# Turning four columns of final sums on VectorE in blocks of 32, with a store of sixteen short runs

## The chip, the cores and the metric

The kernel runs on one core of a Trainium2 chip. The metric is the device time of one execution in microseconds. A core has five engines that run their own programs and wait for one another through semaphores: PE (TensorE, matrix products and transposes), DVE (VectorE), ACT (ScalarE), POOL (GpSimd) and SP (SyncE, which here issues most of the transfers). Sixteen DMA engines move data between the memory (HBM) and the on-chip memory SBUF; PE writes its results to a second on-chip memory, PSUM.

## The reference

One decoding step of a layer with two branches, mixed by a gate g. Branch a is attention of one new position over a cache of 4096 positions with 32 heads of 128; branch b is a small network with a squared ReLU. Everything is bfloat16.

```python
def _A_ref(x, k_cache, v_cache, wq, wo):      # x: 1 x 1 x 512, caches: 1 x 32 x 4096 x 128
    q = (x @ wq).reshape(B, Sq, Hq, Dh) ...
    scores = jnp.einsum("bhqd,bhkd->bhqk", q, k) * (Dh ** -0.5)
    p = _softmax(scores, axis=-1)
    o = jnp.einsum("bhqk,bhkd->bhqd", p, v)
    return ... @ wo                            # 4096 -> 512
def _B_ref(x, w1, b1, w2, b2):
    h = x @ w1 + b1                            # 512 -> 1376
    r = jnp.where(h > 0, h, 0)
    return (r * r) @ w2 + b2                   # 1376 -> 512
g = _sigmoid((x * gate_w).sum(-1, keepdims=True))
return g * a + (1 - g) * b                     # 1 x 1 x 512
```

## The kernel before

The heads are handled in eight groups of four (q = 0 to 7). For each group SP loads 4 MB of keys and 4 MB of values into two slots each, in an order that is written out by hand (ORDER); the weights wq, w1, wo and w2 are put between them. Twelve of every 32 key blocks are multiplied and summed on DVE (L685, L689); the others are transposed on PE (L460), copied out by ACT (L355) and multiplied on PE (L467). ACT computes the exponentials (L372), PE the products with the values (L501). PE's program is a loop of named pieces with branches.

The 512 outputs are summed in `acc`, four columns of 128 partitions in PSUM: output number 128 j + p stands in column j of partition p. The output projection (`out_rows`, L534) and the second layer of the network (`mlp_out`, L545) add to these columns with one matmul for each column and each block of weights. The last piece of w2 to be needed is the last load that SP issues, and the store waits behind it on SP.

The end of the kernel, which the change touches, is one line of steps. DVE adds the bias columns b2g to acc and writes `accs`, 128 x 4 in bfloat16 (L756). PE transposes accs into four rows of 128 in PSUM, `acc4` (L646). DVE copies these to SBUF, `fin4` (L758). SP, which waits for that at L281, stores fin4 as four rows of 256 B from partitions 0 to 3 (L282). After the block of the engines' programs has ended (L760), SP waits for the store to land (L761), and the program is over. The semaphores on the way are s_acc (last matmul done), s_as (accs written), s_fin (transposed), s_f4 (fin4 written) and s_out (stored).

Of the kernel before, what the change touches and what calls it, by code (L numbers as in the profile page):

```python
# [5 lines left out]
def bass_gated_mix__gqa_block_cached__dense_activation_squared_relu__decode_kernel(  # L6
# [16 lines left out]
    bf16 = mybir.dt.bfloat16  # L23
# [56 lines left out]
    with ctx:  # L80
        def sb(name, shape, dt):
            return ctx.enter_context(nc.sbuf_tensor(name, shape, dt))

        def pb(name, shape, dt):
            return ctx.enter_context(nc.psum_tensor(name, shape, dt))

        def sem(name):
            return ctx.enter_context(nc.semaphore(name))
# [21 lines left out]
        b2r = w1_sb[0:4, 2, 0:128]  # L110
        oT = sb("oT", [GH, 128], bf16)
        o2 = sb("o2", [128, TB], bf16)
        fin4 = sb("fin4", [4, 128], bf16)
        zeros = sb("zeros", [128, 128], bf16)
        xb = sb("xb", [128, 4, 128], bf16)
        ident = sb("ident", [128, 128], bf16)
# [21 lines left out]
        accs = sb("accs", [128, 4], bf16)  # L138
# [4 lines left out]
        pO = pb("pO", [128, 512], fp32)  # L143
# [7 lines left out]
        O2 = KP[3][:, 0:2 * TB].bitcast(fp32)  # L151
        Z = pO[:, 76:77]
        B2 = pO[:, 78:80].bitcast(bf16)
        acc4 = pO[0:4, 128:192].bitcast(bf16)
        QR = [pQ[:, :]] + [p[:, :].bitcast(fp32) for p in KP[0:3]] + [pQ[:, :]] * (NQ - QF)
        H = KP[0][:, 0:2 * (FG + 1)].bitcast(fp32)
        acc = pQ[:, 256:260]
# [53 lines left out]
        s_oc = sem("s_oc")  # L211
        s_acc = sem("s_acc")
        s_as = sem("s_as")
        s_fin = sem("s_fin")
        s_f4 = sem("s_f4")
        s_out = sem("s_out")

# [11 lines left out]
        @block.sync  # L229
        def _(eng):  # L230
            def load_kv(n):
                kind, q = ORDER[n]
                if q >= 2:
                    done(kind, q - 2)
                if kind == "K":
                    eng.dma_start(KV[:, K_SLOT[q], :], k_q[q, :, :]).then_inc(s_k[q], 16)
                else:
                    at = 0
                    for m, sv in zip(V_PARTS[q], s_v[q]):
                        a, b = at * PB * 128, (at + m) * PB * 128  # L240
                        eng.dma_start(KV[:, V_SLOT[q], a:b], v_q[q, :, a:b]).then_inc(sv, 16)  # L241
                        at += m

            def done(kind, q):
                if kind == "K":
                    eng.wait_ge(s_sd, NP * (q + 1))
                    eng.wait_ge(s_t, GQ * (q + 1))
                else:
                    eng.wait_ge(s_pv, q + 1)

            def load_wo(g):
                if g == 0:
                    eng.wait_ge(s_qps, NQ)
                elif g < NG - 1:
                    eng.wait_ge(s_wd, g)
                a = 0 if g < NG - 1 else 1
                eng.dma_start(wo_sb[:, a, :, :], wo_v[g, :, :, :]).then_inc(s_wo[a], 16)  # L257

            def load_w2(n):
                a, b = W2_PARTS[n]  # L260
                if a < FG:
                    eng.dma_start(w2a[:, a:b, :], w2_v[:, a:b, :]).then_inc(s_w2[n], 16)  # L262
                else:
                    eng.dma_start(w2b[:, :], B_w2[FG * 128:F, :]).then_inc(s_w2[n], 16)  # L264

            for n in range(len(ORDER)):
                load_kv(n)
                if n == 2:
                    eng.wait_ge(s_z, 1)
                    eng.wait_ge(s_b2, 1)  # L270
                    eng.dma_start(w1_sb[:, :, :], w1_v[:, :, :]).then_inc(s_w1, 16)
                if n in WO_AT:
                    load_wo(WO_AT[n])
            load_wo(NG - 1)
            eng.wait_ge(s_sd, NP * NQ)
            load_w2(0)
            load_w2(1)
            load_w2(2)
            load_w2(3)
            load_w2(4)  # L280
            eng.wait_ge(s_f4, 1)  # L281
            eng.dma_start(out[0, 0, :].rearrange("(j p) -> j p", p=128), fin4[:, :]).then_inc(s_out, 16)  # L282


        @block.gpsimd
# [122 lines left out]
        def _(eng):  # L408
# [129 lines left out]
            def mlp_out(c, last=False):  # L538
                eng.wait_ge(s_w2[c], 16)
                a, b = W2_PARTS[c]  # L540
                for n in range(a, b):
                    M = 128 if n < FG else FR
                    w = w2a[:, n, :] if n < FG else w2b[:, :]
                    for j in range(4):
                        mm = eng.matmul(acc[:, j:j + 1], w[:, j * 128:(j + 1) * 128], hs[0:M, n:n + 1],  # L545
                                        start=False, stop=last, skip_group_check=True)
                if last:
                    mm.then_inc(s_acc, 1)
# [93 lines left out]
            mlp_out(2)  # L642
            mlp_out(3)
            mlp_out(4, last=True)
            eng.wait_ge(s_as, 1)
            eng.transpose(acc4, accs[:, :], ident[:, :]).then_inc(s_fin, 1)  # L646


        @block.vector
        def _(eng):  # L650
# [103 lines left out]
            eng.wait_ge(s_acc, 1)  # L754
            eng.wait_ge(s_bg, 1)
            eng.tensor_tensor(accs[:, :], acc[:, 0:4], b2g[:, :], ALU.add).then_inc(s_as, 1)  # L756
            eng.wait_ge(s_fin, 1)
            eng.tensor_copy(fin4[:, :], acc4).then_inc(s_f4, 1)  # L758

        body.close()  # L760
        nc.sync.wait_ge(s_out, 16)  # L761
# [28 lines left out]
```

## Time and profile before

| what | value |
|---|---|
| time, median of 3 runs | 190.87 us (190.75 to 190.93) |
| time of the profiled execution | 190.55 us |
| its span | 189.2 us |
| mean granted TensorE clock | 0.735 |
| busy: PE, DVE, ACT, POOL | 137.1, 123.0, 116.0, 6.0 us |
| DMA | 78.47 MB, mean 415 GB/s |
| packets under 512 B, of all | 483 of 4177 |

The span runs from the first to the last instruction of the profiled execution; its device time is 1.35 us longer. Busy times of engines overlap and don't add up to the span. In the profile's lines a step is named by the line of the kernel, the engine, and the tiles that it writes and reads; buffer numbers are left out, so fin4 is shown as fin.

### The profile page before, as it was taken

How to read it: one execution, taken by the hardware profiler on the slowest of the kernel's cores; microseconds unless marked ns; L12 is line 12 of the kernel's file. 1: busy time of each engine (PE TensorE's matmuls, PEld its weight loads, DVE VectorE, ACT ScalarE, POOL GpSimd, SP SyncE). 2: the span in 40 equal slices, each digit the busy share in tenths (PEclk: the TensorE clock that was granted, in tenths of full speed). 3: DMA queues.
4: the chain of work that ended last, by engine and by line, in shares of the span. 5: the costliest groups of instructions: out<-in, count | busy, mean ns of one | idle time of the engine just before them, and what ended most of it. 6: DMA issues, size and time to landing. Idle time of an engine off the chain costs nothing. (4 is left out here: it accounts for less than half of the span.)

```text
span 189.2 us, 6234 instructions
## 1 busy us (share of the span) xinstructions
PE 137.1 (72%) x2688; PEld 119.8 (63%) x2688; DVE 123.0 (65%) x123; ACT 116.0 (61%) x243; POOL 6.0 (3%) x13
## 2 busy tenths in 40 slices
PE   0009297668849979969968797829868496889865
PEld 0003165537739779758958696829767495879864
DVE  0110099979969999996998299919990499701010
ACT  3004559948989986984987099708973298560000
POOL 4000000000700000000000000000000000000000
PEclk9999969958975975995795559655985579555555
DMA  6999999989989999999999999999999999999992
GB/s 225 437 444 443 443 443 426 443 361 483 440 360 436 443 443 440 417 436 430 443 424 409 423 443 443 436 436 436 414 445 409 416 443 443 438 388 416 421 388 78
DMA packets 4177, 78.47 MB, mean 415 GB/s; under 512 B 483, under 2 KB 837, under 8 KB 1094
## 3 DMA queue, kind: packets, MB, share of 16 engines
q1 hardware_dynamic: 4152, 78.32, 97.1%
q8 instruction: 7, 0.11, 0.2%
q14 instruction: 4, 0.03, 0.0%
q10 hardware_dynamic: 14, 0.01, 0.0%
HBM read 78.32 MB, written 0.00 MB: 414 GB/s over the span
## 5 line engine op out<-in xcount | busy, mean ns | idle before, releaser
L355 ACT ACTIVATE kT<-KP 128x1024 bf16<-128x1024 bf16 x80 | 75.3, 1041 | 26.1 <-PE KP L460 25.9
L685 DVE TENSOR_TENSOR w2a<-KV,qb 128x1536 f32<-128x1536 bf16 x32 | 56.3, 1760 | 19.4 <-DMA KV<-in_A_k_cache_dram 19.0
L460 PE MATMUL KP<-ident,KV 128*128 128x128 bf16 x640 | 59.6, 256 | 10.5 <-PEq L455 10.5
L460 PEld LDWEIGHTS KP<-ident,KV 128*128 128x128 bf16 x640 | 48.4, 116 | 14.1 <-issue 13.1
L689 DVE TENSOR_REDUCE S<-w2a 128x12 f32<-128x1536 f32 x32 | 56.1, 1753 | 1.1
L467 PE MATMUL pS<-qc,kT 128*128 128x4 bf16 x640 | 28.1, 166 | 13.0 <-PEq L455 11.0
L467 PEld LDWEIGHTS pS<-qc,kT 128*128 128x128 bf16 x640 | 24.6, 99 | 18.9 <-issue 17.6
L501 PEld LDWEIGHTS pO<-E,KV 128*128 128x128 bf16 x1024 | 29.3, 105 | 0.0
L501 PE MATMUL pO<-E,KV 128*128 128x4 bf16 x1024 | 28.4, 166 | 0.0
L372 ACT ACTIVATE E<-S,nM 32x128 bf16<-32x128 f32 x32 | 18.5, 578 | 0.9
L445 PE MATMUL pQ<-W,xb 128*128 128x512 bf16 x20 | 7.8, 532 | 7.2 <-DMA W<-in_A_wq_dram 6.1
L338 ACT ACTIVATE qb<-pQ 32x128 bf16<-32x128 f32 x20 | 5.4, 268 | 9.7 <-PE pQ L445 9.3
L361 ACT ACTIVATE S<-pS 32x80 f32<-32x80 f32 x32 | 7.3, 228 | 4.8 <-PE pS L467 4.2
L445 PEld LDWEIGHTS pQ<-W,xb 128*128 128x128 bf16 x20 | 2.2, 126 | 9.6 <-DMA W<-in_A_wq_dram 6.2
L372 ACT ACTIVATION_READ_ACCUMULATOR E<-S,nM 32x1 f32 x32 | 8.1, 252 | 0.0
L664 DVE TENSOR_SCALAR e<-ez 128x1 f32<-128x1 f32 x1 | 0.2, 153 | 10.8 <-ACT ez L387 10.8
L708 DVE RECIPROCAL rden<-pO 128x4 f32<-128x4 f32 x8 | 1.4, 174 | 8.2 <-PE pO L501 8.2
L594 PE MATMUL pO<-ident,w_sb 1*128 1x1 bf16 x4 | 0.3, 165 | 7.8 <-DMA w_sb<-in_A_x_dram 7.8
L497 PE MATMUL pO<-RS,onesf 128*128 128x4 f32 x16 | 4.3, 339 | 1.8 <-PEq L455 1.8
L655 DVE TENSOR_SCALAR xb<-zeros,xcolf 128x128 bf16<-128x128 bf16 x4 | 0.7, 248 | 7.5 <-ACT xcolf L331 7.5
L488 PE MATMUL pM<-identf,mp 128*1 128x128 f32 x8 | 3.0, 372 | 3.4 <-PEq L455 3.1
L497 PEld LDWEIGHTS pO<-RS,onesf 128*128 128x128 f32 x16 | 3.8, 298 | 2.1 <-issue 2.0
(75 smaller groups left out, 72.2 us busy)
## 6 DMA issues: line engine op xcount, KB each, us to landing
KV<-in_A_k_cache_dram SPq DMA_DIRECT2D x8, 4096.0 KB, 22.0
KV<-in_A_v_cache_dram SPq DMA_DIRECT2D x7, 4096.0 KB, 29.5
W<-in_A_wq_dram SPq DMA_DIRECT2D x1, 4096.0 KB, 13.4
W<-in_A_wo_dram SPq DMA_DIRECT2D x4, 1024.0 KB, 16.5
KV<-in_A_v_cache_dram SPq DMA_DIRECT2D x1, 2048.0 KB, 11.0
KV<-in_A_v_cache_dram SPq DMA_DIRECT2D x2, 1024.0 KB, 14.1
w_sb<-in_B_w_dram SPq DMA_DIRECT2D x1, 1376.0 KB, 24.4
w2a<-in_B_w_dram SPq DMA_DIRECT2D x2, 512.0 KB, 18.5
```

Of the source, the lines that this page charges most:

```text
L338: eng.activation(qb[rows(r), c, :], QR[c][rows(r), r * 128:(r + 1) * 128], ACT.Copy)\
L355: eng.activation(kT[:, n % NT, :], KP[n % NKP][:, :], ACT.Copy).then_inc(s_ev, 1)
L361: eng.activation(S[rows(r), q % NS, 0:YQ], S2[rows(r), :, r], ACT.Copy).then_inc(s_cp, 1)
L372: eng.activation(E[rows(r), q % 2, :, r], S[rows(r), q % NS, :], ACT.Exp, bias=nM[rows(r), q:q + 1], scale=SCALE, accum_out=RS[rows(r), q ...
L445: mm = eng.matmul(QR[c], xb[:, t, :], wq_sb[:, t, c * 512:(c + 1) * 512], start=(t == 0), stop=(t == 3))
L460: mm = eng.transpose(KP[(GQ * a + g) % NKP][:, y * 128:(y + 1) * 128], key(a, b), ident[:, :])
L467: mm = eng.matmul(pS[:, R * c:R * c + R], kT[:, (GQ * a + g) % NT, y * 128:(y + 1) * 128], qc2[:, a, :], start=True, stop=True)
L488: eng.transpose(MT, mp[:, a:a + 1], identf[:, :]).then_inc(s_mt, 1)
L497: eng.matmul(DEN[a], onesf[:, :], RS[:, a, :], start=True, stop=True)
L501: mm = eng.matmul(O[a], KV[:, V_SLOT[a], b * 128:(b + 1) * 128], E[:, a, COLUMN[b], :], start=(b == 0), stop=(b == NB - 1))
L685: eng.tensor_tensor(prod, KV[:, K_SLOT[q], x:x + XB * 128].rearrange("p (b d) -> p b d", d=128), qb[:, q, :].unsqueeze(1).to_broadcast([12 ...
L689: eng.tensor_reduce(S[:, q % NS, c:c + XB], prod, AX.X, ALU.add).then_inc(s_sd, 1)
```

## The change

DVE does the turning. It has a transpose of its own that turns each square block of 32 partitions x 32 elements by itself. Its input here is accs with every column read 32 times (an access with a step of zero), which makes 128 partitions x (4 x 32) elements; its output is `fin`, 128 x 128. After it, every partition of block a (partitions 32 a to 32 a + 31) holds, for each column j, the 32 values that stood in column j of that block's partitions. Of these equal rows one for each block is stored: partitions 0, 32, 64 and 96. Each holds four pieces of 32 outputs (64 B) that belong at four places of the output, 256 B apart, so the store consists of 16 runs. The transpose on PE, its semaphore s_fin, the PSUM columns acc4 and the copy to fin4 are gone.

```diff
-        fin4 = sb("fin4", [4, 128], bf16)
+        fin = sb("fin", [128, 128], bf16)
...
-        acc4 = pO[0:4, 128:192].bitcast(bf16)
...
-        s_fin = sem("s_fin")
...
             eng.wait_ge(s_f4, 1)
-            eng.dma_start(out[0, 0, :].rearrange("(j p) -> j p", p=128), fin4[:, :]).then_inc(s_out, 16)
+            eng.dma_start(out[0, 0, :].rearrange("(j k i) -> k j i", j=4, k=4),
+                          fin[0:128:32, :].rearrange("k (j i) -> k j i", j=4)).then_inc(s_out, 16)
...
             mlp_out(4, last=True)
-            eng.wait_ge(s_as, 1)
-            eng.transpose(acc4, accs[:, :], ident[:, :]).then_inc(s_fin, 1)
...
             eng.tensor_tensor(accs[:, :], acc[:, 0:4], b2g[:, :], ALU.add).then_inc(s_as, 1)
-            eng.wait_ge(s_fin, 1)
-            eng.tensor_copy(fin4[:, :], acc4).then_inc(s_f4, 1)
+
+            eng.wait_ge(s_as, 1)
+            eng.transpose(fin[:, :].rearrange("p (j i) -> p j i", j=4),
+                          accs[:, :].rearrange("p (j a) -> p j a", a=1).broadcast_to([128, 4, 32]))\
+               .then_inc(s_f4, 1)
```

## The prediction

> **What bounds the kernel now.** I read the page first, for what ended last, then the chain in order of time, then the timeline of the last two microseconds, then the waits of SP, and last the DVE rows from which an unseen operation can be priced.
>
> The page says that the kernel as a whole is held by its loads: the 16 DMA engines are at nine tenths in nearly every slice until the last. The chain that ended last confirms it, and it shows what lies behind the last load:
>
> ```profile
> 168.56 18.33 DMA w2a<-in_B_w_dram
> 186.90 0.05 issue
> 186.94 0.28 PE pQ L545 x4
> 187.22 0.02 issue
> 187.25 0.17 DVE accs L756
> 187.42 0.04 issue
> 187.46 0.28 PE pO L646
> 187.75 0.02 issue
> 187.77 0.21 DVE fin L758
> ```
>
> Columns: start, length, what ran. The last piece of w2 lands at 186.90, and from there each step waits for the one before: four matmuls, the sum on DVE (L756), the PE transpose (L646), the DVE copy (L758). The change lies wholly inside this stretch. Nothing overlaps it, so here a saved nanosecond is a nanosecond of the span.
>
> Does the store wait for just this copy, and does anything else end later? The waits of SP answer:
>
> ```profile
> SPq L282 <- DVE fin L758: 18.3, 1, 18.3
> SPq L761 <- DMA out_dram<-fin: 0.5, 1, 0.5
> ```
>
> SP has stood at the store (L282) for 18.3 us and is released by the copy; at the end it waits 0.5 us for the store alone. The store's issue, in the timeline, and windows around its packets:
>
> ```profile
> 188.01 0.33 SPq L282 DMA_DIRECT2D out_dram<-fin  x1
> ```
>
> ```profile
> 188.00:188.75 0.75, 0.00 (x0) 0.00 (x0) 0.00 (x0) 0.00 (x0) 0.00 (x0) 0.50 0.00 0
> 188.75:188.80 0.05, 0.00 (x0) 0.00 (x0) 0.00 (x0) 0.00 (x0) 0.00 (x0) 0.50 0.08 16
> 188.80:188.85 0.05, 0.00 (x0) 0.00 (x0) 0.00 (x0) 0.00 (x0) 0.00 (x0) 0.50 0.04 5
> 188.85:189.20 0.35, 0.00 (x0) 0.00 (x0) 0.00 (x0) 0.00 (x0) 0.00 (x0) 0.50 0.00 0
> ```
>
> The last two columns are the DMA engines' share and GB/s. From the issue at 188.01 it takes 0.74 us until packets move, they move for at most 0.10 us, and then 0.35 us pass with nothing in them until the span ends at 189.2. So the 1.2 us of the store are nearly all fixed time, and only 0.10 us are packets.
>
> **Part by part: the turn of the sums.** Removed: from the end of L756 (187.25 + 0.162 = 187.41) to the issue of the store (188.01) pass 0.60 us. They are 0.05 to PE, 0.27 for L646 (at the granted clock of 0.50 that the windows show), 0.04 to DVE, 0.21 for L758, 0.03 to SP.
>
> Added in its place: a wait of DVE for its own sum, one block transpose of 128 partitions x 128 elements (four columns, each read 32 times), and the 0.03 to SP. Behind the waiting transpose nothing is queued on DVE, and only the store waits for it. A dependent pair on DVE with the same kind of wait is L708 and L716: in the timeline the first starts at 182.03, takes 0.18 and the second starts at 182.25, a gap of 0.04.
>
> The trace has no DVE transpose, so I bound it by its neighbours (mean ns of one is the number after the comma):
>
> ```profile
> L689 DVE TENSOR_REDUCE S<-w2a 128x12 f32<-128x1536 f32 x32 | 56.1, 1753 | 1.1
> L694 DVE TENSOR_REDUCE mp<-S 128x1 f32<-128x128 f32 x8 | 2.3, 286 | 2.9 <-ACT S L361 2.3
> L701 DVE TENSOR_SCALAR dg<-gm 1x128 f32<-1x128 f32 x8 | 1.7, 215 | 0.3
> L655 DVE TENSOR_SCALAR xb<-zeros,xcolf 128x128 bf16<-128x128 bf16 x4 | 0.7, 248 | 7.5 <-ACT xcolf L331 7.5
> ```
>
> L701 is the lower end: it reads each of four columns 32 times, just the pattern of the change, in 0.215 us; so reading a column again and again is not dear in itself. L694 and L689 give the rate of an operation that takes elements one at a time: (1753 - 286) / (1536 - 128) = 1.04 ns an element, so 286 - 133 = 0.153 us fixed and 0.133 us for 128 elements. A square block of 32 must have its 32 columns in before its first row can go out, which adds 32 x 1.04 = 0.033: 0.286 + 0.033 = 0.32 us if filling and emptying overlap from block to block. If each block is emptied before the next is filled, it is 0.153 + 2 x 0.133 = 0.42 us, the upper end. I take 0.31, near the one-at-a-time row, because a transpose has to move single elements between partitions.
>
> The Trainium skill ("VectorE: DVE Perf Modes", section "The three transpose paths") gives 311 ns for a 128x128 bf16 block transpose on VectorE, beside 390 ns on TensorE; no run here shows the former, the trace has L646 at 268 ns, and by the page's figure the new step would come out at the same 0.31.
>
> New stretch: 0.04 + 0.31 + 0.03 = 0.38 us against 0.60: **0.22 us saved**, with the bounds 0.60 - (0.07 + 0.215) = 0.31 and 0.60 - (0.07 + 0.42) = 0.11.
>
> **Part by part: the store.** It has the same 1 KB, but 16 runs of 64 B in place of four of 256 B, from partitions 0, 32, 64, 96 in place of 0 to 3. Three terms. Issue: the store with four rows took 0.334 us on SP, and the load of 96 rows (L264) 0.43 in the timeline; (0.43 - 0.334) / 92 is 1 ns a row, so 12 runs more cost 0.01 us. A pattern of two nested steps is not in the trace; if it is issued as dearly as 96 rows, it is 0.10. Packets: (0.08 + 0.04) x 16 x 0.05 = 0.096 us of DMA engine time, over four rows 0.024 us each, the completion write included. If each further run costs as much as that whole, a queue of four has 3 x 0.024 = 0.07 us more; if short runs cost by their bytes, 0. I take 0.03, since a quarter of the bytes can hardly cost the whole. Landing: the empty 0.35 us behind the packets is the write being confirmed; it does not depend on bytes as far as these windows can show, so I take 0.01 more, with bounds of 0 and of three such waits one behind the other (the slow rival below). Reading from four far apart partitions could also shorten the packets, at best by their whole 0.10 us. Sum: **0.05 us lost**, with bounds of a gain of 0.10 and a loss of some 1.2.
>
> **The rest.** The scratch in PSUM and one semaphore go, PE's program ends two steps earlier, fin has the same 256 bytes a partition. PE has no work behind L646 that anything waits for, so its cost is nothing with or without cover. The loads up to 186.90 are not touched.
>
> **Sum.** -0.22 + 0.05 = -0.17 us. The profiled execution took 190.55 us (span 189.2, 1.35 around it), which would become 190.38. It lies 0.32 below the median of the three runs, 190.87, so executions differ by more than the sum is worth; the difference is carried to the median: **190.70 us**. A measurement of this kernel can tell about 0.2% from no change, 0.38 us: below 190.49 or above 191.25. The forecast gain is 0.09%, less than that: I forecast no difference that can be told.
>
> **Rival one, slower: the short runs of the store are confirmed one after another.** Its place is the stretch from the first packet to the last release. Four engines write 64 B pieces side by side into each 256 B of the output, so every piece has neighbours that others write in the same moment, and a piece that has to read and put back its surroundings would wait for them. The price is the empty 0.35 us for each further piece of a queue: with all three in line 3 x 0.35 = 1.05, less the 0.22 saved, plus 0.01 for the issue: 190.87 + 0.84 = 191.71; with two in line 191.36. It decides from 0.60 us of additional store on (0.22 + 0.38). For it: the store is the last link and wholly uncovered. Against it: four rows now move in one burst, with a single wait behind them, so writes of different queues do not line up there. The Trainium skill ("DMA: Bandwidth & Descriptors", section "Specifications") puts line rate at 512 B and more and says that below it the DMA engine reads, modifies and writes; no run here shows it. Chance 0.20.
>
> **Rival two, faster than can be overlooked.** The transpose costs what L701 costs (0.215), because the pattern is the same, and the packets from four separate partitions get shorter. Then 0.31 are saved, up to 0.41 with the whole 0.10 of the packets: 190.56 to 190.46. For it: the pattern is in the trace at that price. Against it: L701 runs over one partition and moves nothing between partitions, and most of the range stays above 190.49. Chance 0.20, of which 0.14 beyond the bound.
>
> **Rival three: the gain is eaten at the issue.** Issue 0.10, packets 0.07 and the transpose at 0.42: -0.11 + 0.17 = +0.06, 190.93. Also not to be told from no change. Chance 0.10. That the change might touch nothing on the end's path is excluded by the chain, which holds both removed steps.
>
> **How the numbers follow.** Forecast 0.50 (its own range 190.56 to 190.85), rival one 0.20, rival two 0.20, rival three 0.10. Faster: the 0.14 of rival two. Slower: the 0.20 of rival one. Same: 0.50 + 0.10 + 0.06 = 0.66. The range goes down to 190.45, the end of rival two, and up to 191.35, rival one with two waits in line; what it leaves out is above all three in line, and so under 0.2.
>
> **What would show it.** In the changed profile the end of the chain should read: DVE sum, a gap of 0.04, a DVE transpose of 0.28 to 0.34, an issue of the store within 0.38 us of the sum's end, 0.33 to 0.36 long, packets over at most 0.15 us, an empty 0.35 behind them. A transpose over 0.42 or under 0.215 breaks the first term; an end more than 1.3 us behind the store's issue breaks the second, and over 1.8 proves rival one's size. If DVE shows other instructions beside the one transpose, or the last load no longer ends near 186.9, the forecast is wrong in what it left out.

## The result and the profile after

The change makes the kernel slower: 191.26 us median (190.99 to 192.62, 19 runs) against 190.86 us (19 runs of before beside it), ratio 1.0026 with a 95% interval of 1.0014 to 1.0038. That is 0.40 us between the medians, inside the range of the prediction and just beyond the 0.38 us that can be told. The forecast of no difference, with a small gain, has the wrong sign.

The profiled execution of after took 191.16 us with a span of 189.7. Its last stretch, from the timeline (start, length, engine, line, operation):

```profile
187.47 0.16 DVE L753 TENSOR_TENSOR accs<-pQ,b2g 128x4 bf16<-128x4 f32 x1 [3.23 <-PE pQ L544]
187.67 0.31 DVE L756 STREAM_TRANSPOSE fin<-accs 128x128 bf16<-128x128 bf16 x1
188.01 0.69 SPq L280 DMA_DIRECT2D out_dram<-fin  x1
```

The sum starts 0.22 us later than in before (187.47 against 187.25), because the matmuls in front of it, which wait for the last loads, started 0.27 us later in this execution (186.33 against 186.06), and yet the store is issued at the same 188.01: the turn takes 0.54 us from the sum's start where it took 0.76. The transpose is the one instruction that was foreseen. But the issue of the store, 0.33 us before, now takes 0.69. SP waits for the same two things as before, at the same two places:

```profile
SPq L280 <- DVE fin L756: 18.1, 1, 18.1
SPq L761 <- DMA out_dram<-fin: 0.4, 1, 0.4
```

The windows around the store's packets (start and end of the window, its length, busy time of five engines, granted clock, DMA share, GB/s), for after:

```profile
188.00:189.28 1.28, 0.00 (x0) 0.00 (x0) 0.00 (x0) 0.00 (x0) 0.00 (x0) 0.50 0.00 0
189.28:189.40 0.12, 0.00 (x0) 0.00 (x0) 0.00 (x0) 0.00 (x0) 0.00 (x0) 0.50 0.09 9
189.40:189.75 0.35, 0.00 (x0) 0.00 (x0) 0.00 (x0) 0.00 (x0) 0.00 (x0) 0.50 0.00 0
```

The packets move for about 0.1 us and the empty time behind them is 0.35 us, both as before. The loss lies ahead of the first packet: 1.27 us from the issue in place of 0.75, that is 0.52 us more, of which 0.35 is in the issue itself (685 ns against 334) and 0.17 between its end and the first packet. With the 0.22 us that the turn saves this makes 0.30 us of loss, where the medians differ by 0.40 and the interval reaches from 0.27 to 0.73 us. The spans of the runs agree with the 0.30: their median is 189.8 in after and 189.5 in the runs of before that stood beside e1 and e7 below. The other 0.1 us would then lie outside the span: device time less span is 1.46 us (median) in after and 1.47 in e1, which has the same source partitions, against 1.38 and 1.39 in those runs of before. What happens there the trace does not show.

So the landing of the short runs, rival one, is not where the time went. Three things about the new store were left to be told apart: its sixteen runs in a nested pattern, its source partitions, and the DVE transpose that goes ahead of it.

### The profile page after: what moved, and what is told of

It reads as the page before. It is cut to its first block, busy times and chain, and to the rows that moved or that the text cites. A ratio compares the mean times of both kernels' runs of the same rounds, so it can differ in the third digit from the quotient of the medians.

```text
span 189.7 us, 6229 instructions
## 1 busy us (share of the span) xinstructions
PE 136.7 (72%) x2684; PEld 118.7 (63%) x2687; DVE 123.1 (65%) x123; ACT 115.9 (61%) x243; POOL 6.0 (3%) x13
## 5 line engine op out<-in xcount | busy, mean ns | idle before, releaser
L459 PE MATMUL KP<-ident,KV 128*128 128x128 bf16 x640 | 58.0, 251 | 10.0 <-PEq L454 9.9
L459 PEld LDWEIGHTS KP<-ident,KV 128*128 128x128 bf16 x640 | 47.2, 114 | 13.6 <-issue 12.5
L466 PEld LDWEIGHTS pS<-qc,kT 128*128 128x128 bf16 x640 | 23.9, 98 | 20.0 <-issue 18.1
L444 PE MATMUL pQ<-W,xb 128*128 128x512 bf16 x17 | 6.7, 528 | 7.7 <-DMA W<-in_A_wq_dram 6.3
```

The costliest lines, as they stand in the source:

```text
L444: mm = eng.matmul(QR[c], xb[:, t, :], wq_sb[:, t, c * 512:(c + 1) * 512], start=(t == 0), stop=(t == 3))
L459: mm = eng.transpose(KP[(GQ * a + g) % NKP][:, y * 128:(y + 1) * 128], key(a, b), ident[:, :])
L466: mm = eng.matmul(pS[:, R * c:R * c + R], kT[:, (GQ * a + g) % NT, y * 128:(y + 1) * 128], qc2[:, a, :], start=True, stop=True)
```

## The experiments

In the diffs, lines with a plus stand in place of the store of the kernel named.

**Runs or partitions, from both sides.** e1 keeps the partitions of the change and goes back to four whole rows; e2 keeps the turn and the partitions of before and takes sixteen runs.

```diff
 # e1_rows4, from after
+ eng.dma_start(out[0, 0, :].rearrange("(k f) -> k f", k=4), fin[0:128:32, :])
 # e2_pe16, from before
+ eng.dma_start(out[0, 0, :].rearrange("(k j i) -> j k i", j=4, k=4),
+               fin4[:, :].rearrange("j (k i) -> j k i", k=4))
```

> The block transpose of the change, with the store of before: four whole rows of 256 B, now from partitions 0, 32, 64, 96, to four adjoining places (so the pieces of the output stand in another order). If the loss is the number of runs or the nested pattern of the store: its issue on SP takes 0.33 us again, the first packet comes 0.74 us behind the issue, and only the 0.22 us of the turn are left: 0.22 us faster than before, ratio near 0.9988. If the loss comes from reading four partitions that lie far apart: the issue stays near 0.69 and the kernel is slower than before by 0.3 us, ratio 1.0016.

> The kernel before (PE transpose, DVE copy), with a store of 16 runs of 64 B from partitions 0 to 3 (each row of 256 B is cut in four pieces that go to places 256 B apart, so the output stands in another order). If runs or the nested pattern cost: issue 0.69 us, first packet 1.27 us behind it, in all 0.53 us slower than before, ratio 1.0028. If far apart partitions cost: issue 0.33 us and no difference from before.

e1: 191.19 us, ratio 1.0027 (1.0011 to 1.0042), as slow as the change with four runs only. e2: 190.85 us, ratio 1.0002 (0.9994 to 1.0011), as fast as before with sixteen. The stores of both in the timeline, e1 first:

```profile
188.02 0.64 SPq L280 DMA_DIRECT2D out_dram<-fin  x1
```

```profile
188.44 0.35 SPq L282 DMA_DIRECT2D out_dram<-fin  x1
```

First packets came 1.22 us and 0.76 us behind the issue. My theory ahead of these two was that runs cost; both refute it. Sixteen runs of 64 B cost at most 0.02 us at the issue.

**More or fewer runs.** The same question by a series, on the changed kernel with j runs a partition (2 in e4, 8 in e5; the change has 4).

```diff
+ eng.dma_start(out[0, 0, :].rearrange("(j k i) -> k j i", j=2, k=4),     # 8 in e5_runs32
+               fin[0:128:32, :].rearrange("k (j i) -> k j i", j=2))
```

> The changed kernel with two runs of 128 B for each of the four partitions, eight runs in all, the pattern nested as in the change (output in another order). If each run costs: from four runs (0.33) to sixteen (0.69) is 0.030 us a run, so the issue takes 0.45 us, and the first packet comes 0.74 + 4 x 0.044 = 0.92 us behind it. If the nesting costs a fixed sum: issue 0.69 and 1.27, as with sixteen runs.

> The changed kernel with eight runs of 32 B for each of the four partitions, 32 in all (output in another order). If each run costs: issue 0.33 + 28 x 0.030 = 1.17 us, first packet 0.74 + 28 x 0.044 = 1.97 us behind it. If the nesting costs a fixed sum: issue 0.69 us, first packet at 1.27.

These two, and e6, e8, e9 and e13 below, were run once each, so only the lengths in their profiles are read. The stores in the timeline, e4 first:

```profile
187.83 0.69 SPq L280 DMA_DIRECT2D out_dram<-fin  x1
```

```profile
188.12 0.68 SPq L280 DMA_DIRECT2D out_dram<-fin  x1
```

The first packet came 1.27 and 1.28 us behind the issue: no dependence on the number of runs from 8 to 32. Taken alone this fits "the nesting costs a fixed sum", but e1 has no nesting and 0.64, and e2 is nested and has 0.35. Between e1 and the nested stores there may be 0.05 us that belong to the nesting.

**Partitions or transpose.** e7 keeps the transpose and reads partitions 0 to 3; e8 reads 0, 2, 4, 6; e9 has the PE transpose and reads 0, 32, 64, 96.

```diff
 # e7_first4, from after
+ eng.dma_start(out[0, 0, :].rearrange("(k f) -> k f", k=4), fin[0:4, :])
 # e8_step2, from after
+ eng.dma_start(out[0, 0, :].rearrange("(k f) -> k f", k=4), fin[0:8:2, :])
 # e9_pe_far, from before
-fin4 = sb("fin4", [4, 128], bf16)
+fin4 = sb("fin4", [128, 128], bf16)
+ eng.dma_start(out[0, 0, :].rearrange("(j p) -> j p", p=128), fin4[0:128:32, :])
```

> The block transpose of the change, and a store of four whole rows of 256 B from partitions 0 to 3 instead of 0, 32, 64, 96 (all four hold block 0, so three quarters of the output are left out). If the long issue comes from the partitions (their step or their distance): issue 0.34 us, first packet 0.74 us behind it, and the kernel is 0.22 us faster than before, ratio 0.9988. If it comes from the DVE transpose that goes ahead or from the wide tile: issue 0.69 us and 0.3 us slower than before, ratio 1.0016.

> As e7_first4, but from partitions 0, 2, 4, 6: a step of two, all in one quarter of the partitions. If any step other than one makes the issue long: 0.69 us, first packet 1.27 us behind it. If only partitions in different quarters do: issue 0.34 us, first packet at 0.74.

> The kernel before (PE transpose, DVE copy) with a tile of 128 partitions behind it, of which partitions 0, 32, 64, 96 are stored, each as one row of 256 B (three of them hold zeros that are written at the start, so three quarters of the output are left out). If the partitions make the issue long: 0.69 us, and the end comes 0.5 us later than before behind the copy. If the DVE transpose does: issue 0.34 us, as before.

The timelines, e7, e8 and e9 in this order:

```profile
187.45 0.16 DVE L752 TENSOR_TENSOR accs<-pQ,b2g 128x4 bf16<-128x4 f32 x1 [3.33 <-PE pQ L543]
187.65 0.31 DVE L755 STREAM_TRANSPOSE fin<-accs 128x128 bf16<-128x128 bf16 x1
187.99 0.33 SPq L280 DMA_DIRECT2D out_dram<-fin  x1
```

```profile
187.74 0.74 SPq L280 DMA_DIRECT2D out_dram<-fin  x1
```

```profile
188.07 0.64 SPq L282 DMA_DIRECT2D out_dram<-fin  x1
```

e7 has the short issue (first packet at 0.75 us) with the DVE transpose ahead of it: 190.58 us, ratio 0.9986 (0.9977 to 0.9995), by the ratio 0.27 us faster than before. That is the gain of the turn by itself, predicted as 0.22. e9 has the long issue (first packet at 1.23) without any DVE transpose. And e8 has it (first packet at 1.32) within one quarter of the partitions, a step of two being enough. So it is neither the transpose nor the distance: a source whose partitions are not adjoining is issued more slowly. The windows of e7 and e1, which differ in the source partitions alone, show that nothing else differs; e7 first:

```profile
187.99:188.74 0.75, 0.00 (x0) 0.00 (x0) 0.00 (x0) 0.00 (x0) 0.00 (x0) 0.50 0.00 0
188.74:188.84 0.10, 0.00 (x0) 0.00 (x0) 0.00 (x0) 0.00 (x0) 0.00 (x0) 0.50 0.06 10
188.84:189.20 0.36, 0.00 (x0) 0.00 (x0) 0.00 (x0) 0.00 (x0) 0.00 (x0) 0.50 0.00 0
```

```profile
188.02:189.24 1.22, 0.00 (x0) 0.00 (x0) 0.00 (x0) 0.00 (x0) 0.00 (x0) 0.50 0.00 0
189.24:189.34 0.10, 0.00 (x0) 0.00 (x0) 0.00 (x0) 0.00 (x0) 0.00 (x0) 0.50 0.06 10
189.34:189.70 0.36, 0.00 (x0) 0.00 (x0) 0.00 (x0) 0.00 (x0) 0.00 (x0) 0.50 0.00 0
```

Only the first window differs, by 0.47 us.

**Fixed or by the partition.** Sixteen partitions with a step of eight, and two with a step of 32.

```diff
 # e6_parts16, from after
+ eng.dma_start(out[0, 0, :].rearrange("(q i) -> q i", q=16), fin[0:128:8, 0:32])
 # e13_two, from after
+ eng.dma_start(out[0, 0, :].rearrange("(k f) -> k f", k=4)[0:2, :], fin[0:64:32, :])
```

> The changed kernel, but its store takes 16 partitions with a step of eight, one run of 64 B from each (only the first column's pieces, each of them four times, so three quarters of the output are left out). If a step other than one costs a fixed sum: issue 0.64 to 0.74 us as with four partitions, first packet 1.25 us behind it. If it costs by the partition (0.30 us for four is 0.08 for each): issue 0.33 + 16 x 0.08 = 1.5 us, first packet 2 us behind it.

> The changed kernel, but only partitions 0 and 32 are stored, one row of 256 B each (half of the output is left out). If a step other than one costs a fixed sum: issue 0.64 to 0.74 us, first packet 1.25 us behind it. If it costs by the partition: issue near 0.48 us, first packet at 1.0.

The stores in the timeline, e6 first:

```profile
188.03 0.56 SPq L280 DMA_DIRECT2D out_dram<-fin  x1
```

```profile
188.01 0.61 SPq L280 DMA_DIRECT2D out_dram<-fin  x1
```

The first packet came 1.21 us behind the issue in both. The price does not grow with the partitions: 0.5 us or so per store, with two as with sixteen. It is not quite the same for every pattern (the issue took 0.56 us with a step of eight, 0.61 to 0.69 with 32 and 0.74 with two), and why is open.

**No turn at all.** If the number of runs costs nothing at the issue, the sums could go out as they stand.

```diff
 # e10_direct, from before, without transpose and copy; SP waits for s_as
+ eng.dma_start(out[0, 0, :].rearrange("(j p) -> p j", p=128), accs[:, :])
```

> No turn at all: the sums are stored as they stand, 128 adjoining partitions with four single elements each, 512 runs of 2 B. The issue then follows the sum by 0.03 us, which saves 0.57 us of the turn of before. If the issue depends on partitions and not on runs (8, 16 and 32 runs took the same): issue 0.43 us as for other loads of 128 rows, 0.1 us more than before; 32 packets on each of 16 engines, at 7 ns a packet some 0.2 us more. In all 0.25 us faster than before, ratio 0.9987. If runs of 2 B have to read and put back what stands around them, one behind the other: slower by the empty 0.33 us behind the packets for each of them that has to wait, 1 us and more.

203.40 us, ratio 1.0656 (1.0640 to 1.0673). The issue is short (0.40 us) and follows the sum at once; the packets are not the cost either:

```profile
187.82:188.40 0.58, 0.00 (x0) 0.00 (x0) 0.00 (x0) 0.00 (x0) 0.00 (x0) 0.50 0.00 0
188.40:190.00 1.60, 0.00 (x0) 0.00 (x0) 0.00 (x0) 0.00 (x0) 0.00 (x0) 0.50 0.16 1
190.00:202.10 12.10, 0.00 (x0) 0.00 (x0) 0.00 (x0) 0.00 (x0) 0.00 (x0) 0.50 0.00 0
```

A finer window, behind which all are empty, shows the end of the packets, and SP's waits show what it stands for at the end:

```profile
189.10:189.20 0.10, 0.00 (x0) 0.00 (x0) 0.00 (x0) 0.00 (x0) 0.00 (x0) 0.50 0.04 0
```

```profile
SPq L758 <- DMA out_dram<-accs: 13.4, 1, 13.4
```

The packets are all gone by 189.2, and then 12.9 us pass in which nothing moves that the trace shows, until the store is confirmed. The second expectation had the way, with "1 us and more", and not the size. So the time to the confirmation can grow, as rival one had it, but with 512 runs of 2 B, not with 16 or 32 runs of 64 or 32 B. Whether the length or the number of the runs does it was not separated, and how the 12.9 us come about can't be seen here.

**A version without the step.** All 32 partitions of a block hold the same row. Partitions 31 and 32 are therefore as good as 0 and 32, and 95 and 96 as good as 64 and 96, and each of these pairs adjoins.

```diff
 # both from after; e11_pairs: store(eng, 0) on SP, store(eng, 1) on ACT, which waits for s_f4
 #                  e12_pairs_sp: both on SP, one behind the other
+def store(eng, h):
+    eng.dma_start(out_k[2 * h:2 * h + 2], fin_k[64 * h + 31:64 * h + 33]).then_inc(s_out, 16)
-nc.sync.wait_ge(s_out, 16)
+nc.sync.wait_ge(s_out, 32)
```

(out_k and fin_k are the two views of out and fin that the change's store has.)

> The changed kernel, output in full and in order, with its store in two halves: since all 32 partitions of a block hold the same row, partitions 31 and 32 hold blocks 0 and 1, and 95 and 96 blocks 2 and 3, each pair with a step of one. SP issues the first pair, ACT the second, both behind the transpose, eight runs of 64 B each. If the step of the partitions alone makes the issue long: both issues take 0.33 us or less side by side, first packets 0.75 us behind them, and 0.22 to 0.27 us are saved, as in e7_first4: ratio 0.9987. If crossing from one quarter of the partitions to the next makes it long: issues near 0.69, and 0.3 us slower than before, ratio 1.0016.

> As e11_pairs, but SP issues both pairs, one behind the other. If the step of the partitions alone makes the issue long: the second issue starts 0.35 us behind the first, takes 0.33 us, and its packets come 0.75 us behind its own start: 0.35 us later than in e11_pairs, so 0.1 us slower than before, ratio 1.0005. If crossing the quarters does: 0.69 twice, 1.0 us slower than before.

e11: 190.59 us, ratio 0.9992 (0.9983 to 1.0002). e12: 190.89 us, ratio 1.0008 (0.9999 to 1.0017). Beside the change's 1.0026 (1.0014 to 1.0038), e11 is clearly faster; e12's interval still touches that of the change. Against before neither is told from no difference, and e11's gain, 0.15 us by the ratio, is smaller than the 0.27 of e7, with intervals that overlap. In e11's timeline the issues are short and stand side by side, as foreseen:

```profile
187.48 0.31 DVE L763 STREAM_TRANSPOSE fin<-accs 128x128 bf16<-128x128 bf16 x1
187.82 0.33 SPq L231 DMA_DIRECT2D out_dram<-fin  x1
187.82 0.27 ACTq L231 DMA_DIRECT2D out_dram<-fin  x1
```

The first packet is 0.76 us behind. But the windows show something new at the end:

```profile
187.82:188.58 0.76, 0.00 (x0) 0.00 (x0) 0.00 (x0) 0.00 (x0) 0.00 (x0) 0.50 0.00 0
188.58:188.66 0.08, 0.00 (x0) 0.00 (x0) 0.00 (x0) 0.00 (x0) 0.00 (x0) 0.50 0.15 13
188.66:189.20 0.54, 0.00 (x0) 0.00 (x0) 0.00 (x0) 0.00 (x0) 0.00 (x0) 0.50 0.00 0
```

The empty time is 0.54 us where the stores of four partitions by SP alone had 0.35 to 0.38. In e12 the same two halves, both from SP, have their last packets at 189.02 and the span's end at 189.4, so the halves as such do not land late. This is one profile of each. Whether it is the second queue, or two stores at the same moment, was not separated.

## Why the prediction was wrong

**The turn was right.** The transpose took 0.313 us in after; the estimate by the one-at-a-time row, 0.31, and the figure of the Trainium skill ("VectorE: DVE Perf Modes", section "The three transpose paths", 311 ns) agree with it. The stretch from the sum's end to the store's issue was 187.47 + 0.162 to 188.01, which is 0.38 us, the forecast figure. e7 shows the gain in whole times: 0.27 us with an interval of 0.10 to 0.44.

**The term that failed is the issue of the store.** It was priced by its rows, 0.01 us, with 0.10 as the upper bound, and the time from the issue's end to the first packet was taken as fixed. The two grew by 0.35 and 0.17. The bound was made from a load of 96 adjoining partitions; no transfer of before has a source or destination with a partition step other than one, so the price of such a step was not in the trace, and I did not see that it was missing. The reading behind the 0.01, 1 ns a row, does not hold either: most of the key loads in the same trace (L236, 128 rows) were issued in 0.33 us, like the store of four rows, so the 0.43 of L264 did not come from its rows. I did look at the four far apart partitions, but only as a chance for the packets to get shorter, and set them down on the side of gain. The unknown I did name, the nested pattern, turned out to cost some 0.05 us at most (e1 against e4, e5 and after). That the time lies inside the stated range is luck: the upper end of the range came from rival one.

**Packets and landing were right.** Packets 0.10 to 0.12 us, empty time 0.35 to 0.38, for 4, 16 and 32 runs. Rival one had the sign, and the time where it ended (191.36 with two waits in line) was near, but its mechanism is refuted by e2: sixteen runs of 64 B land like four of 256 B. The rule of the Trainium skill that stood beside it ("DMA: Bandwidth & Descriptors", section "Specifications": below 512 B the engine reads, modifies and writes) draws no line between 64 B and 256 B, and neither do these runs. That section gives no price for runs of 2 B, and no run shows whether reading and putting back is what takes the 12.9 us in e10.

**Rival two** needed the transpose at 0.215 us and shorter packets; neither came. Its chance did not fit its own range either: 0.14 of its 0.20 was put beyond 190.49, though most of 190.56 to 190.46 lies above that. **Rival three** had the right place, the issue, with a third of the price that was measured and another cause, the nested steps; with the 0.52 us that was measured, in place of 0.10 + 0.07, it would have come out as slower.

**The chances.** Slower had 0.20, all of it on a mechanism that does not act with runs of 64 B. The prediction's own test, "an end more than 1.3 us behind the store's issue breaks the second" (the store's term), is what the trace met: 189.7 - 188.01 = 1.7.

## What to carry to other kernels

Price a store by the address pattern of its source as well, not by its bytes and runs alone, and check whether the trace already holds a transfer of that pattern; if not, its issue is an unknown of its own. (Only the source side of a store was tested here, not the destination of a load.) Where a result is repeated over partitions, choose the copies that adjoin: partitions 31 and 32 served where 0 and 32 had cost half a microsecond. Cutting a small store into runs of 32 or 64 B is cheap, cutting it into 512 single elements of 2 B was not.

## What the runs showed of the hardware

- A store whose source partitions have a step other than one took 0.56 to 0.74 us to issue on SP in place of 0.33 to 0.35, and its first packet came 1.21 to 1.32 us behind the start of the issue in place of 0.75 (after, e1, e4 to e6, e8, e9 and e13 against before, e2 and e7). All of 2, 4 and 16 partitions, steps of 2, 8 and 32, and 2 to 32 runs lie in this band; what spreads them inside it is open.
- From 4 to 32 runs, 256 B to 32 B long, from the same partitions, neither the issue nor the landing of a 1 KB store grew by more than 0.05 us (e1, e4, e5 and after; before and e2). With 512 runs of 2 B the store was confirmed 12.9 us after the last packet (e10).
- Two halves of a store from SP and ACT at the same time ended 0.54 us behind the last packet (e11, one profile), where a store of four partitions from SP alone took 0.35 to 0.38; the cause is open.
- A DVE transpose that reads each of four columns 32 times took 0.313 us in after. The estimate from the rows of L689 and L694, with the filling of one block, was 0.32; that the transpose works this way inside is not shown.
